# ScalarE of the first mixer product in hand-set order, and the sums of the fourth moving operand in three places

## The chip, the cores and the metric

The kernel runs on one core of one Trainium2 chip. The time is device microseconds (us) of one execution; the figure quoted is the median of several executions. The core has a matrix engine (TensorE, PE in the profile; its weight loads are listed apart as PEld), a vector engine (VectorE, DVE), a scalar engine (ScalarE, ACT), GpSimd (POOL), and DMA queues, of which this kernel mostly uses the one issued from SyncE (SP). Each engine runs its own stream of instructions; where one needs another's result it waits on a semaphore. Matmul results stand in PSUM, which has eight banks of 128 x 512 32-bit numbers. All other tiles stand in SBUF.

## The reference

```python
def _A_ref(x, wqkv, wo):              # linear attention, 32 heads of 32
    q, k, v = ...x @ wqkv...
    phi = lambda t: jnp.where(t > 0, t + 1, jnp.exp(t)) + 1e-6
    pq, pk = phi(q), phi(k)
    kv = jnp.einsum("bhsd,bhse->bhde", pk, v)
    z = jnp.einsum("bhsd->bhd", pk)
    num = jnp.einsum("bhqd,bhde->bhqe", pq, kv)
    den = jnp.einsum("bhqd,bhd->bhq", pq, z)[..., None] + 1e-6
    return (num / den ...) @ wo

def _B_ref(x, w1, b1, w2, b2):        # token-mixing MLP
    h = _layernorm(x, axis=-1)
    u = _gelu(jnp.einsum("bsd,sf->bdf", h, w1) + b1)
    y = jnp.einsum("bdf,fs->bds", u, w2) + b2
    return y.transpose(0, 2, 1)

h = x + _A_ref(_layernorm(x), A_wqkv, A_wo)
out = h + _B_ref(_layernorm(h), B_w1, B_b1, B_w2, B_b2)
```

x is 2048 x 1024 (S x D), w1 is 2048 x 3584 (S x F), w2 is 3584 x 2048, all bf16. The change lies in "mixer 1", the product of w1 with the normalized h and its gelu.

## The kernel before

The program runs attention, then mixer 1, then mixer 2. In the trace mixer 1 lies between about 235 and 400 us. Its moving operand h is kept in SBUF as hE and hO, the even and odd blocks of 128 rows, each 128 x 8 x 1024 in fp16; gelu(u) goes to gE and gO in the same form.

**Seven products in place of eight.** A pair of 128-wide column blocks of w1 is one `Mixer1`. It computes a 2 x 2 block matrix product with seven block products `p1` to `p7` (512 columns each) instead of eight. The stationary sides of products 5, 6, 7 and 3 are sums of blocks of w1, made on VectorE (tiles `sa`, method `asums`); the moving sides 2 to 7 are differences of blocks of hE and hO. The accumulators A, B, C and E are chained: B starts as a copy of A, C as a copy of B, so one engine copies PSUM to PSUM between the products.

**The same once more inside.** Two `Mixer1` form a `Quad`. Products 1, 5, 2 and 3 of the two are again a 2 x 2 block product, and are done by an `Inner` (or `Inner2`, which adds its results to a base already in SBUF): seven products `i1` to `i7`, of four matmuls of 256 columns each. I call the four inners of a quad in1, in5, in2 and in3, in the order in which they run. Their stationary sums are the tiles `is`; their moving sums come from `inner_moving`, where `sums1`, `sums5`, `sums2` and `sums3` each make four 128 x 1024 differences on VectorE, once for the whole of mixer 1: in order, moving sides 7, 5 (in place), 6 and 4. In an inner, PSUM slices a, b, c and e are chained thus: `i1` fills a; ScalarE copies a to b (line 258); `i6` adds to b; ScalarE copies b to c (line 262); `i2` adds to a, which is a result; `i5` fills e; `i7` adds to c, a result; `i3` adds to b, a result; `i4` adds to c once more, a result, after the result of `i7` has been read out of c. Results go through a `sink`: for in1 ScalarE copies to the base t1a and to the PSUM tile B (lines 493 and 494) or VectorE adds and ScalarE copies to B (499); for in5 ScalarE or VectorE writes the shared tile e (502); for in2 and in3 VectorE adds to the base tiles t1a and t (`t3` in the code).

**Interleaving.** `interleave(n, steps, at)` emits an inner n, and between its products it fills in matmuls of 512 columns from a list of steps: the previous quad's product 4 during in1, this quad's products 6 (in5, start of in2) and 7 (rest of in2, in3). A filler that ends a product puts its evacuation (`copy_c`, line 362; gelu, line 419; the VectorE add of e and then gelu) into a list `late`, which is emptied after `i7` and at the end of the inner. Named points in between (`in`, `mid`, `third`, `out`) let the caller emit sums and gelus.

A quad u is one call of `run1`. u runs from 1 to 6; quad 0 is `run_first`, which does its products 1, 2, 7 and 3 whole and only product 5 by an inner. `sums3` is called in u = 1 alone, whole, by `before_third()`, just ahead of in2's interleave and the add into the first base of product 3.

**What sets the order.** Instructions whose call is wrapped by `pin` (`tc.keep_in_program_order`) stay in program order on their engine; for all others a planner chooses the place in their engine's stream. `Held(engine)` wraps an engine so that its calls are pinned while `Held.on` is true. Before the change `dve` and `pe` are such wrappers, and in mixer 1 all matmuls and VectorE instructions are pinned. The ScalarE calls of mixer 1 go to `nc.scalar` and are placed by the planner.

PSUM has four pools of two banks: psw (inner e and c, and A of products 1 and 2), psx (B), psy (C), psz (E, and the inner a and b). w1 comes over the SP queue, one tile of 2 x 1024 KB for each quad, two tiles in flight, and at the end come the first tiles of w2.

Of the kernel before, what the change touches and what calls it, by code (L numbers as in the profile page):

```python
# [10 lines left out]
P = 128  # L11
F32 = mybir.dt.float32
# [10 lines left out]
BANK = 512  # L23
# [7 lines left out]
def kernel(  # L31
# [12 lines left out]
    nc = tc.nc  # L44
# [5 lines left out]
    CW = min(BANK, D)  # L50
# [34 lines left out]
    pin = tc.keep_in_program_order  # L85
# [51 lines left out]
    HW = CW // 2  # L137
# [69 lines left out]
        return {1: b11, 2: b21, 3: b22, 4: t4, 5: b12, 6: t2, 7: t3}, sums  # L207

    class Held:
        on = False  # L210

        def __init__(self, engine, always=False):
            self.engine, self.always = engine, always

        def __getattr__(self, name):
            op = getattr(self.engine, name)
            return (lambda *a, **kw: pin(op(*a, **kw))) if self.always or Held.on else op  # L217

    dve, pe = Held(nc.vector), Held(nc.tensor)
    hv, ht, hs, hd = (Held(e, True) for e in (nc.vector, nc.tensor, nc.scalar, nc.sync))  # L220

    class Inner:
        banks = 4

        def __init__(self, sts, m, mov, tag, sink, sink_sum):
            self.nk, self.mov, self.tag = sts[0].nk // 2, mov, tag
# [23 lines left out]
        def i1(self):  # L250
            ae = psz.tile([P, BANK], F32, tag="z0", bufs=1, name="psI0")
            bc = psz.tile([P, BANK], F32, tag="z1", bufs=1, name="psI1")
            e, c = ae, bc
            if self.banks == 4:
                e, c = (psw.tile([P, BANK], F32, tag="w", name=f"psI{i}") for i in (2, 3))
            self.a, self.e, self.b, self.c = ae[:, 0:HW], e[:, HW:CW], bc[:, 0:HW], c[:, HW:CW]
            self.mm(1, self.a, True)
            nc.scalar.copy(self.b, self.a)  # L258

        def i6(self):  # L260
            self.mm(6, self.b, False)
            nc.scalar.copy(self.c, self.b)

        def i2(self):
            self.mm(2, self.a, False)
# [2 lines left out]
        def i5(self):  # L268
            self.mm(5, self.e, True)
            self.es = cpool.tile([P, HW], F32, tag="es", name="es")  # L270
            nc.scalar.copy(self.es[:], self.e)

        def i7(self):
            self.mm(7, self.c, False)
# [5 lines left out]

        def i4(self):
            self.mm(4, self.c, False)
            self.sink(1, 0, self.c)

    class Inner2(Inner):
        def i5(self):
# [11 lines left out]
    class Product7:  # L298
# [45 lines left out]
        def p1(self):  # L344
            self.begin()
            self.mm(1, self.A, True)
            nc.scalar.copy(self.B[:], self.A[:])

        def shared_tile(self):
            self.e = cpool.tile([P, BANK], F32, tag=f"e{self.p % 2}", name="e1")  # L350
# [1 line left out]
        def p5(self, ks=None):  # L352
            if ks is None or ks[0] == 0:
                self.E = psz.tile([P, BANK], F32, tag=f"z{self.p % 2}", bufs=1, name="psE1")
            self.mm(5, self.E, True, ks)
            if self.whole(ks):
                self.shared_tile()
                nc.scalar.copy(self.e[:], self.E[:])

        def copy_c(self):  # L360
            self.C = psy.tile([P, BANK], F32, tag="y", name="psC1")
            nc.scalar.copy(self.C[:], self.B[:])  # L362

        def p6(self, ks=None, late=None):
            self.mm(6, self.B, False, ks)
# [20 lines left out]
        def p7(self, cut=None):  # L386
            self.mm(7, self.C, False)
            self.parts = [(0, CW, self.C)]
            if cut is not None:
                self.parts = [(0, cut, self.C), (cut, CW, psw.tile([P, BANK], F32, tag="w", name="psC2"))]  # L390
                nc.scalar.copy(self.parts[1][2][:, cut:CW], self.C[:, cut:CW])
            self.evac_shared(1, self.C)

        def p3(self):
# [17 lines left out]
    class Mixer1(Product7):  # L412
# [3 lines left out]

        def evac(self, fh, dh, ps, a=0, b=CW):
            ft = 2 * self.p + fh
            nc.scalar.activation(
                (gE if fh == 0 else gO)[:, self.p, dh * CW + a:dh * CW + b],  # L420
                ps[:, a:b], ACT.Gelu_apprx_tanh, bias=b1_sb[:, ft:ft + 1], scale=1.0,
            )
# [9 lines left out]
        todo = []  # L432
# [49 lines left out]
    class Quad:  # L482
# [7 lines left out]

        def sink1(self, m, h, ps):
            A, B, c = self.sts[m].A, self.sts[m].B, self.cols(h)
            nc.scalar.copy(A[:, c], ps)
            nc.scalar.copy(B[:, c], A[:, c])

        def sum1(self, m, h, ps, es):
            A, B, c = self.sts[m].A, self.sts[m].B, self.cols(h)
            dve.tensor_tensor(A[:, c], ps, es, ALU.add)
            nc.scalar.copy(B[:, c], A[:, c])

        def sink5(self, m, h, ps):
            nc.scalar.copy(self.sts[m].e[:, self.cols(h)], ps)

        def sum5(self, m, h, ps, es):
            dve.tensor_tensor(self.sts[m].e[:, self.cols(h)], ps, es, ALU.add)
# [1 line left out]
        def steps(self, *fs):  # L507
            return [(f, k) for f in fs for k in range(self.sts[0].nk)]

        def interleave(self, n, steps, at={}):  # L510
            t = len(steps)
            cuts = [0, (5 * t + 8) // 16, (9 * t + 8) // 16, (12 * t + 8) // 16, t]

            late = []

            def fill(q):
                for f, part in groupby(steps[cuts[q]:cuts[q + 1]], lambda s: s[0]):
                    f([k for _, k in part], late)

            def flush():  # L520
                while late:
                    late.pop(0)()

            for f in (
                n.i1, "in", 0, n.i6, n.i2, 1, n.i5, n.i7, flush, 2, "mid", n.i3, "third", 3, n.i4, "out", flush,
            ):
                if isinstance(f, int):
                    fill(f)
                else:
                    (at.get(f, nop) if isinstance(f, str) else f)()  # L530

        def asums(self, m):
            if not isinstance(self.sts[0], Mixer1):
# [97 lines left out]
                dve.tensor_tensor(base[:, m, c], ps, base[:, m, c], ALU.add)  # L631
            return sink

        def run1(self, pend, nxt, on_p4, before_third=nop):
            sts = self.sts
            s4, s6, s7 = self.steps(*[st.p4 for st in pend]), self.steps(*[st.p6 for st in sts]), self.steps(*[st.p7_fill for st in sts])
            c6, c7 = 3 * len(s6) // 4, len(s7) // 2

            def starting():
                self.in1.sums(slice(2, 4))  # L640
                self.asums(5)
                self.in5 = Inner(sts, 5, self.mov5, "i5", self.sink5, self.sum5)
                self.in5.sums(slice(0, 2))
                self.asums(6)
                self.t1 = self.base("t1a")
                for s, st in enumerate(sts):
                    st.begin(self.t1[:, s, :])

            self.interleave(self.in1, s4, {"in": starting, "mid": lambda: self.in5.sums(slice(2, 4))})
            self.asums(7)  # L650
            in2 = Inner2(sts, 2, self.mov2, "i1", self.add_to(self.t1), None)
            in2.sums()
            on_p4()
            nxt = nxt()
            for st in sts:
                st.shared_tile()
            self.interleave(self.in5, s6[:c6])
            sts[0].finish()
            self.asums(3)
            self.base3()  # L660
            in3 = Inner2(sts, 3, self.mov3, "i5", self.add_to(self.t3), None)
            in3.sums()
            before_third()
            sts[0].with_shared(sts[0].base3, sts[0].B)
            self.interleave(in2, s6[c6:] + s7[:c7], {
                "third": lambda: sts[0].evac(0, 0, sts[0].A), "out": lambda: sts[1].evac(0, 0, sts[1].A),
            })
            sts[1].with_shared(sts[1].base3, sts[1].B)
            if nxt is not None:
                nxt.begin1()  # L670
            self.interleave(in3, s7[c7:], {
                "third": lambda: sts[0].evac(0, 1, sts[0].base3), "out": lambda: sts[1].evac(0, 1, sts[1].base3),
            })
            return sts, nxt

    def moving(E, O, T2, T3, T4):
# [11 lines left out]
    with ExitStack() as actx:  # L688
# [21 lines left out]
        with ExitStack() as a1:  # L710
# [455 lines left out]
            for q in range(2, NVP):  # L1166
                for R in (KRun, VRun):
                    n = R(q)
                    i = 2 * q + 3 if R is KRun else 2 * q + 4
# [27 lines left out]
            for b in range(NKB):  # L1197
                j0, n = b * KPB, min(KPB, ND - b * KPB)
# [28 lines left out]
        with ExitStack() as a3:  # L1227
# [143 lines left out]
            for n, (u, j) in enumerate(q_units[8:]):  # L1371
# [14 lines left out]
                if n in sums_at:  # L1386
                    cur = next(ahead)
# [44 lines left out]
    psw = ctx.enter_context(tc.tile_pool(name="psw", bufs=NT, space=PSUM, reuse_waits="tile"))  # L1432
# [13 lines left out]
    mov3, sums3 = inner_moving(hO[:, :, CW:D], NSP, inner1, "hi3")  # L1446
    NQ1 = NFP // 2

    def next_load1(u):
        def load():  # L1450
            if u < NQ1:
                load_w1(u, 0)
                load_w1(u, 1)
            else:
                load_w2(0, wpool)
        return load

    def quad1(u):
        return Quad([Mixer1(2 * u), Mixer1(2 * u + 1)], mov1, mov5, mov2, mov3)

    Held.on = True
    sums5()
    cur.mov5 = mov5
    pend, nxt = cur.run_first(quad1(1), sums1, sums2)
    for u in range(1, NQ1):
        cur = nxt
        pend, nxt = cur.run1(pend, lambda: quad1(u + 1) if u + 1 < NQ1 else None, next_load1(u + 1), sums3 if u == 1 else nop)
    Held.on = False
    for st in pend:
        st.p4()  # L1470
    mctx.close()
# [11 lines left out]
    cur = Mixer2(0)  # L1483
# [42 lines left out]
    pend = [cur, Mixer2(1)]  # L1526
    nxt = quad2(1)
# [26 lines left out]
    for u in range(1, NSP // 2):  # L1554
        cur = nxt
        last = 2 * u + 2 == NSP
# [35 lines left out]
```

## Time and profile before

| | us |
|---|---|
| median of 8 runs | 570.06 |
| lowest and highest | 568.27, 570.83 |
| the profiled execution | 570.83 |
| its span, first to last instruction | 569.0 |
| TensorE busy in the span | 560.0 |
| VectorE busy | 431.7 |
| ScalarE busy | 280.9 |

A row of a timeline gives the start of a group of like instructions and its length in us, the engine, the line of the code, the operation, the tile written and those read, the shape, the count, and in brackets how long the engine stood idle before it and what it waited for. Line 217 is the helper that pins, so all pinned matmuls and VectorE instructions have that line and are told apart by their tiles. In in1 to in3 the moving side is hE (in1, in5) or hO (in2, in3), or a sum `hi`; the stationary side is wq (the tile of w1), `sa` or `is`. A matmul's own duration is a latency: of matmuls in a row, those of 512 columns start about 0.217 us apart and those of 256 about 0.109 us apart. The clock of TensorE in a row of a window is 1.00 at full speed.

### The profile page before, as it was taken

The page shows a single profiled execution, that of the slowest core. Times are in us where ns is not written, and L with a number is a line of the kernel's source. Part 1 is how long each engine was busy: PE and PEld are TensorE (multiplying, and loading weights), DVE is VectorE, ACT ScalarE, POOL GpSimd, SP SyncE. Part 2 cuts the span into 40 slices and gives each one's busy share as a digit, 9 for nine tenths or more (in the row PEclk, how much of TensorE's full clock was granted, in tenths as well). Part 3 has the DMA queues.
Part 4 walks back from the last instruction along what each step waited for, and adds up shares of the span by engine and source line. Part 5 has one row for each costly group of instructions (what it writes and reads, how often), then busy time and mean ns, then how long its engine had stood idle before and what let it go on. Part 6 is the DMA issues. An engine that isn't in the chain of part 4 may idle for free.

```text
span 569.0 us, 8564 instructions
## 1 busy us (share of the span) xinstructions
PE 560.0 (98%) x3215; PEld 304.6 (54%) x3215; DVE 431.7 (76%) x822; ACT 280.9 (49%) x597; POOL 1.8 (0%) x8
## 2 busy tenths in 40 slices
PE   8999999999999999999899999999999999999997
PEld 3444444454444444456566666666445655645643
DVE  6898888543785788878889789887989749658725
ACT  4747677757766877635355455464220411311211
POOL 1000000000000000000000000000000000000000
PEclk9999999999999999999899999999999999999999
DMA  9833332125773851104040440413892932912111
GB/s 300 292 75 74 83 85 38 19 66 190 206 217 110 273 181 74 56 0 148 2 149 1 149 127 23 149 55 77 218 245 89 248 90 74 288 47 74 38 47 46
DMA packets 86089, 67.15 MB, mean 118 GB/s; under 512 B 15762, under 2 KB 80032, under 8 KB 86048
## 3 DMA queue, kind: packets, MB, share of 16 engines
q1 hardware_dynamic: 85312, 65.94, 40.3%
q10 hardware_dynamic: 672, 0.66, 0.3%
q8 instruction: 25, 0.41, 0.3%
q14 instruction: 16, 0.13, 0.1%
q0 software_dynamic: 64, 0.01, 0.0%
HBM read 54.54 MB, written 8.91 MB: 112 GB/s over the span
## 4 chain that ended last, share of the span: by engine, by line
PE 87%; DVE 9%; ACT 2%; issue 1%; ACTq 0%; DVEq 0%
PE acc_t L217 18%; PE psI L217 15%; PE psC L217 11%; PE psB L217 10%; PE psA L217 4%; PE psB L854 4%; PE psC L854 4%; PE psA L854 4%; DVE is L217 3%; PE acc_t L778 3%; PE psA L328 2%; PE acc_t L1129 2%; PE psB L328 2%; PE psE L854 2%; DVE sa L217 2%; PE psC L328 2%
## 5 line engine op out<-in xcount | busy, mean ns | idle before, releaser
L217 PEld LDWEIGHTS <-wq 128*128 128x128 bf16 (+1 forms) x629 | 61.1, 98 | 48.3 <-issue 2.7
L217 PEld LDWEIGHTS <-sa 128*128 128x128 f16 x627 | 61.8, 99 | 36.5 <-issue 0.3
L217 PEld LDWEIGHTS <-is 128*128 128x128 f16 x568 | 55.7, 98 | 28.0 <-issue 2.7
L217 PE MATMUL acc_t<-wo_sb,pqT 128*128 128x512 f16 x256 | 55.6, 379 | 0.0
L217 PE MATMUL psC<-gs,wq 128*128 128x512 f16 (+2 forms) x210 | 44.9, 365 | 0.0
L217 PE MATMUL acc_t<-xnT,wq_sb 128*128 128x512 bf16 x192 | 43.4, 379 | 0.0
L217 PEld LDWEIGHTS <-pqT 128*128 128x128 bf16 x256 | 24.9, 98 | 30.5 <-issue 0.6
L179 DVE TENSOR_SCALAR e_sb<-e_sb 128x512 bf16<-128x512 bf16 x64 | 18.6, 290 | 28.7 <-ACT e_sb L175 28.2
L175 ACT ACTIVATE e_sb<-acc_t 128x512 bf16<-128x512 f32 x40 | 23.9, 597 | 24.6 <-PE acc_t L217 12.0
L854 PEld LDWEIGHTS <-xs 128*128 128x128 f16 x208 | 20.0, 98 | 23.3 <-DVE xs L840 1.3
L217 DVE TENSOR_TENSOR ot<-ot,hr 128x512 bf16<-128x512 bf16 (+2 forms) x27 | 11.2, 414 | 28.1 <-ACT ot L469 27.7
L217 PE MATMUL psC<-hT,sa 128*128 128x512 f16 x112 | 31.9, 386 | 0.0
L217 PE MATMUL psI<-hi,is 128*128 128x256 f16 x200 | 30.5, 275 | 0.8 <-ACT psI L258 0.2
L217 PEld LDWEIGHTS <-wq_sb 128*128 128x128 bf16 x192 | 18.5, 98 | 23.0 <-issue 1.3
L258 ACT COPY psI<-psI 128x256 f32<-128x256 f32 x31 | 11.2, 362 | 39.1 <-PE psI L217 38.3
L217 PE MATMUL psB<-hT,sa 128*128 128x512 f16 x112 | 29.7, 379 | 0.0
L217 DVE BATCH_NORM_STATS2 hst<-acc_t 128x6 f32<-128x512 f32 x32 | 21.4, 692 | 9.1 <-ACT h_bf L217 8.9
L854 PE MATMUL psA<-wkv,xnT 128*128 128x512 bf16 x104 | 26.7, 379 | 0.0
L362 ACT COPY psC<-psB 128x512 f32<-128x512 f32 x22 | 12.5, 570 | 25.6 <-PE psB L217 20.9
L854 PEld LDWEIGHTS <-xnT 128*128 128x128 bf16 x156 | 15.3, 98 | 18.5 <-issue 0.2
L217 PE MATMUL psC<-hT,wq 128*128 128x512 f16 x96 | 24.6, 379 | 0.0
L217 ACT CAST h_bf<-acc_t 128x512 bf16<-128x512 f32 x32 | 18.4, 582 | 11.9 <-PE acc_t L217 11.2
(209 smaller groups left out, 1052.7 us busy)
## 6 DMA issues: line engine op xcount, KB each, us to landing
wq<-in_B_w_dram SPq DMA_DIRECT2D x14, 1024.0 KB, 8.0
wq<-in_B_w_dram SPq DMA_DIRECT2D x8, 1792.0 KB, 10.3
xr<-in_A_x_dram SPq DMA_DIRECT2D x16, 256.0 KB, 5.0
rdb<-rd_dram SPq DMA_DIRECT2D x32, 128.0 KB, 3.9
h_dram<-h_bf SPq DMA_DIRECT2D x16, 256.0 KB, 2.0
hr<-h_dram SPq DMA_DIRECT2D x32, 128.0 KB, 2.6
out_dram<-ot SPq DMA_DIRECT2D x31, 128.0 KB, 1.7
x_sb<-in_A_x_dram SPq DMA_DIRECT2D x15, 256.0 KB, 3.0
```

The costliest lines, as they stand in the source:

```text
L175: pin(nc.scalar.activation(e_sb[:], src, ACT.Exp))
L179: pin(nc.vector.tensor_scalar(e_sb[:], e_sb[:], 1.0, PHI_EPS, ALU.min, ALU.add))
L217: return (lambda *a, **kw: pin(op(*a, **kw))) if self.always or Held.on else op
L258: nc.scalar.copy(self.b, self.a)
L328: pe.matmul(ps[:, cols], lhsT=lhs[:, k, :], rhs=mv(k)[:, cols], start=(start and k == 0), stop=(k == self.nk - 1), skip_group_check=True,)
L362: nc.scalar.copy(self.C[:], self.B[:])
L778: mm = nc.tensor.matmul(pp[:, 0:CW], lhsT=xnT[:, kt, i * P:(i + 1) * P], rhs=wkv[:, kt, c * CW:(c + 1) * CW], start=(kt == 0), stop=(kt == ...
L854: pin(nc.tensor.matmul(ps[:], lhsT=lhs[:, k, :], rhs=rhs[:, k, :], start=(start and k == 0), stop=(k == hk2 - 1), skip_group_check=True,))
L1129: nc.tensor.matmul(qp[:, 0:SW], lhsT=wq_sb[:, kt, j * P:(j + 1) * P], rhs=xnT[:, kt, u * SW:(u + 1) * SW], start=(kt == 0), stop=(kt == ND ...
```

## The change

1. **ScalarE in program order.** `Held` takes a key, and a third wrapper `act` pins ScalarE's calls while `Held.scalar` is true, which is so for mixer 1. Every ScalarE copy and gelu of mixer 1 goes through it.
2. **Where evacuations stand in that order.** `late` becomes one list for all quads, so that what is left at the end of an inner can be emitted in the next. `interleave` takes a table `flush`: at which named points (`b` behind i1, `c` behind i6, `7` behind i7, `end`) how many entries are emitted; None is all. in1 empties it at `b` and `7`; in5 at `b`, `7` and `end`; in2 at `7`; in3 one entry at `b` and the rest at `c`. The sink of in1's `i4` and the gelus that stood at `out` of in2 and in3 are put at the head of the list, and are emitted behind the next inner's i1. What is left after the last quad is emitted ahead of its product 4.
3. **The slice c gets its bank at i6** instead of at i1, so that the previous inner's c can still be read behind the next i1. The number of banks is the same.
4. **sums3 in three places** of u = 1: the first two differences ahead of in5, the third between in2 and the add into the second base of product 3, the fourth at `b` of in3.

The core of the diff:

```diff
-            nc.scalar.copy(self.b, self.a)
+            act.copy(self.b, self.a)
         def i6(self):
             self.mm(6, self.b, False)
-            nc.scalar.copy(self.c, self.b)
+            if self.banks == 4:
+                self.c = psw.tile([P, BANK], F32, tag="w", name="psI3")[:, HW:CW]
+            act.copy(self.c, self.b)
...
         def i4(self):
             self.mm(4, self.c, False)
-            self.sink(1, 0, self.c)
+            last = partial(self.sink, 1, 0, self.c)
+            if self.behind is None:
+                last()
+            else:
+                self.behind.insert(0, last)
...
-        def interleave(self, n, steps, at={}):
+        late = []
+        def interleave(self, n, steps, at={}, flush=(("7", None), ("end", None))):
...
+            def point(name):
+                todo = len(self.late) if flush.get(name, 0) is None else flush.get(name, 0)
+                for _ in range(todo):
+                    self.late.pop(0)()
+                at.get(name, nop)()
             for f in (
-                n.i1, "in", 0, n.i6, n.i2, 1, n.i5, n.i7, flush, 2, "mid", n.i3, "third", 3, n.i4, "out", flush,
+                n.i1, "b", 0, n.i6, "c", n.i2, 1, n.i5, n.i7, "7", 2, n.i3, "third", 3, n.i4, "end",
             ):
...
+            self.in1.behind = self.late
+            self.interleave(
+                self.in1, s4, {"b": starting, "7": lambda: self.in5.sums(slice(2, 4))}, (("b", None), ("7", None))
+            )
...
+            if third_sums is not None:
+                third_sums(slice(0, 2))
+            self.interleave(self.in5, s6[:c6], flush=(("b", None), ("7", None), ("end", None)))
...
-            before_third()
             sts[0].with_shared(sts[0].base3, sts[0].B)
-            self.interleave(in2, s6[c6:] + s7[:c7], {
-                "third": lambda: sts[0].evac(0, 0, sts[0].A), "out": lambda: sts[1].evac(0, 0, sts[1].A),
-            })
+            self.interleave(
+                in2, s6[c6:] + s7[:c7], {"third": gelu(0, 0, self.t1), "end": gelu_late(1, 0, self.t1)}, (("7", None),)
+            )
+            if third_sums is not None:
+                third_sums(slice(2, 3))
             sts[1].with_shared(sts[1].base3, sts[1].B)
             if nxt is not None:
                 nxt.begin1()
             self.interleave(in3, s7[c7:], {
-                "third": lambda: sts[0].evac(0, 1, sts[0].base3), "out": lambda: sts[1].evac(0, 1, sts[1].base3),
-            })
+                "b": nop if third_sums is None else lambda: third_sums(slice(3, 4)),
+                "third": gelu(0, 1, self.t3), "end": gelu_late(1, 1, self.t3),
+            }, (("b", 1), ("c", None)))
```

`run_first` is not in the diff: it keeps the default table, and its evacuations are emitted where they stood, but are now pinned.

More of the change, by code (lines that the diff above doesn't have):

```diff
@@ L209, with __init__ @@
     class Held:
-        on = False
-        def __init__(self, engine, always=False):
-            self.engine, self.always = engine, always
+        on = scalar = False
+        def __init__(self, engine, always=False, key="on"):
+            self.engine, self.always, self.key = engine, always, key
         def __getattr__(self, name):
             op = getattr(self.engine, name)
-            return (lambda *a, **kw: pin(op(*a, **kw))) if self.always or Held.on else op
-    dve, pe = Held(nc.vector), Held(nc.tensor)
+            return (lambda *a, **kw: pin(op(*a, **kw))) if self.always or getattr(Held, self.key) else op
+    dve, pe, act = Held(nc.vector), Held(nc.tensor), Held(nc.scalar, key="scalar")
     hv, ht, hs, hd = (Held(e, True) for e in (nc.vector, nc.tensor, nc.scalar, nc.sync))
@@ L223 @@
         banks = 4
+        behind = None
         def __init__(self, sts, m, mov, tag, sink, sink_sum):
@@ L252, in i1 @@
             bc = psz.tile([P, BANK], F32, tag="z1", bufs=1, name="psI1")
[L253 to L256, printed above, removed]
+            e = psw.tile([P, BANK], F32, tag="w", name="psI2") if self.banks == 4 else ae
+            self.a, self.e, self.b, self.c = ae[:, 0:HW], e[:, HW:CW], bc[:, 0:HW], bc[:, HW:CW]
             self.mm(1, self.a, True)
-            nc.scalar.copy(self.b, self.a)
+            act.copy(self.b, self.a)
         def i6(self):
             self.mm(6, self.b, False)
-            nc.scalar.copy(self.c, self.b)
+            if self.banks == 4:
+                self.c = psw.tile([P, BANK], F32, tag="w", name="psI3")[:, HW:CW]
+            act.copy(self.c, self.b)
         def i2(self):
@@ L270, in i5 @@
             self.es = cpool.tile([P, HW], F32, tag="es", name="es")
-            nc.scalar.copy(self.es[:], self.e)
+            act.copy(self.es[:], self.e)
         def i7(self):
@@ L346, in p1 @@
             self.mm(1, self.A, True)
-            nc.scalar.copy(self.B[:], self.A[:])
+            act.copy(self.B[:], self.A[:])
         def shared_tile(self):
@@ L357, in p5 @@
                 self.shared_tile()
-                nc.scalar.copy(self.e[:], self.E[:])
+                act.copy(self.e[:], self.E[:])
         def copy_c(self):
             self.C = psy.tile([P, BANK], F32, tag="y", name="psC1")
-            nc.scalar.copy(self.C[:], self.B[:])
+            act.copy(self.C[:], self.B[:])
         def p6(self, ks=None, late=None):
@@ L390, in p7 @@
                 self.parts = [(0, cut, self.C), (cut, CW, psw.tile([P, BANK], F32, tag="w", name="psC2"))]
-                nc.scalar.copy(self.parts[1][2][:, cut:CW], self.C[:, cut:CW])
+                act.copy(self.parts[1][2][:, cut:CW], self.C[:, cut:CW])
             self.evac_shared(1, self.C)
@@ L418, in evac @@
             ft = 2 * self.p + fh
-            nc.scalar.activation(
+            act.activation(
                 (gE if fh == 0 else gO)[:, self.p, dh * CW + a:dh * CW + b],
@@ L492, in sink1 @@
             A, B, c = self.sts[m].A, self.sts[m].B, self.cols(h)
-            nc.scalar.copy(A[:, c], ps)
-            nc.scalar.copy(B[:, c], A[:, c])
+            act.copy(A[:, c], ps)
+            act.copy(B[:, c], A[:, c])
         def sum1(self, m, h, ps, es):
@@ L498, in sum1 @@
             dve.tensor_tensor(A[:, c], ps, es, ALU.add)
-            nc.scalar.copy(B[:, c], A[:, c])
+            act.copy(B[:, c], A[:, c])
         def sink5(self, m, h, ps):
-            nc.scalar.copy(self.sts[m].e[:, self.cols(h)], ps)
+            act.copy(self.sts[m].e[:, self.cols(h)], ps)
         def sum5(self, m, h, ps, es):
@@ L508, in steps @@
             return [(f, k) for f in fs for k in range(self.sts[0].nk)]
-        def interleave(self, n, steps, at={}):
+        late = []
+        def interleave(self, n, steps, at={}, flush=(("7", None), ("end", None))):
             t = len(steps)
             cuts = [0, (5 * t + 8) // 16, (9 * t + 8) // 16, (12 * t + 8) // 16, t]
-            late = []
+            flush = dict(flush)
             def fill(q):
                 for f, part in groupby(steps[cuts[q]:cuts[q + 1]], lambda s: s[0]):
[L518 to L522, printed above, removed]
+                    f([k for _, k in part], self.late)
+            def point(name):
[3 more added lines that the diff above has]
+                at.get(name, nop)()
             for f in (
-                n.i1, "in", 0, n.i6, n.i2, 1, n.i5, n.i7, flush, 2, "mid", n.i3, "third", 3, n.i4, "out", flush,
+                n.i1, "b", 0, n.i6, "c", n.i2, 1, n.i5, n.i7, "7", 2, n.i3, "third", 3, n.i4, "end",
             ):
@@ L528, in interleave @@
                     fill(f)
+                elif isinstance(f, str):
+                    point(f)
                 else:
-                    (at.get(f, nop) if isinstance(f, str) else f)()
+                    f()
         def asums(self, m):
@@ L632, in add_to, with run1 @@
             return sink
-        def run1(self, pend, nxt, on_p4, before_third=nop):
+        def run1(self, pend, nxt, on_p4, third_sums=None):
             sts = self.sts
@@ L647, in starting, with gelu, gelu_late @@
                     st.begin(self.t1[:, s, :])
-            self.interleave(self.in1, s4, {"in": starting, "mid": lambda: self.in5.sums(slice(2, 4))})
+            def gelu(s, dh, t):
+                return lambda: sts[s].evac(0, dh, t[:, s, :])
+            def gelu_late(*args):
+                return lambda: self.late.insert(0, gelu(*args))
+            self.in1.behind = self.late
+            self.interleave(
+                self.in1, s4, {"b": starting, "7": lambda: self.in5.sums(slice(2, 4))}, (("b", None), ("7", None))
+            )
             self.asums(7)
@@ L656, in run1 @@
                 st.shared_tile()
-            self.interleave(self.in5, s6[:c6])
+            if third_sums is not None:
+                third_sums(slice(0, 2))
+            self.interleave(self.in5, s6[:c6], flush=(("b", None), ("7", None), ("end", None)))
             sts[0].finish()
@@ L1459, in quad1 @@
         return Quad([Mixer1(2 * u), Mixer1(2 * u + 1)], mov1, mov5, mov2, mov3)
-    Held.on = True
+    Held.on = Held.scalar = True
     sums5()
@@ L1466 @@
         cur = nxt
-        pend, nxt = cur.run1(pend, lambda: quad1(u + 1) if u + 1 < NQ1 else None, next_load1(u + 1), sums3 if u == 1 else nop)
-    Held.on = False
+        pend, nxt = cur.run1(pend, lambda: quad1(u + 1) if u + 1 < NQ1 else None, next_load1(u + 1), sums3 if u == 1 else None)
+    while Quad.late:
+        Quad.late.pop(0)()
+    Held.on = Held.scalar = False
     for st in pend:
```

## The prediction

> **What bounds the kernel.** I read the page first: span, busy time, and the row of the clock.
>
> ```profile
> span 569.0 us, 8564 instructions
> PE 560.0 (98%) x3215; PEld 304.6 (54%) x3215; DVE 431.7 (76%) x822; ACT 280.9 (49%) x597; POOL 1.8 (0%) x8
> ...
> PEclk9999999999999999999899999999999999999999
> ```
>
> TensorE sets the time everywhere in mixer 1: ScalarE at half load can only matter where a matmul waits for it. One slice has a lower clock. So the second view is the waits of TensorE alone (us in total, times, longest):
>
> ```profile
> PE psI L217 <- DVE t1a L217: 2.5, 1, 2.5
> PE acc_t L778 <- ACT xnT L1031: 0.9, 2, 0.5
> PE psI L217 <- ACT psI L258: 0.2, 1, 0.2
> ```
>
> Only the first and the third lie in mixer 1. A matmul's listed length is a latency, so short gaps hide in it; the third view is therefore the timeline of TensorE, in which I compare each start with the pitch of 0.217 us (512 columns) and 0.109 us (256 columns). This is u = 1, in2, and then two windows with their clock, the third number from the end:
>
> ```profile
> 272.56 0.81 PE L217 MATMUL psC<-hT,sa 128*128 128x512 f16 x3
> 275.83 0.60 PE L217 MATMUL psI<-hi,wq 128*128 128x256 f16 x4 [2.46 <-DVE t1a L217]
> ```
> ```profile
> 10.80:13.00 2.20, 2.19 (x11) 1.01 (x12) 1.54 (x6) 2.06 (x6) 0.00 (x0) 1.00 1.07 368
> 276.50:279.70 3.20, 3.20 (x15) 1.76 (x13) 2.34 (x5) 2.31 (x5) 0.00 (x0) 0.50 0.00 0
> ```
>
> i4 of in2 starts 2.62 us late, then TensorE runs 3.2 us at clock 0.50. From the psC matmuls at 272.56 to those at 279.89 it takes 7.33 us; the same stretch of u = 2, 299.71 to 302.75, takes 3.04. This one place costs **4.29 us**. The timeline of VectorE shows why:
>
> ```profile
> 270.85 0.69 DVE L217 TENSOR_TENSOR hi<-hO 128x1024 f16<-128x1024 f16 x1
> ...
> 273.02 0.69 DVE L217 TENSOR_TENSOR hi<-hO,hi 128x1024 f16<-128x1024 f16 x1
> 273.63 0.68 DVE L217 TENSOR_TENSOR t<-psB,e 128x512 f32<-128x512 f32 x1
> 274.23 1.87 DVE L217 TENSOR_TENSOR t1a<-psI,t1a 128x256 f32<-128x256 f32 x4
> ```
>
> The four differences of sums3 (0.72, 0.73, 0.72 and 0.61 us to the next start, 2.78 together) stand ahead of in2's adds, and i4 may not write c before i7's add has read it (275.35 to 275.77; i4 starts 0.05 later).
>
> Each later quad is 22.86 us long and has one gap, at i6 of in5. Here u = 3, TensorE and then ScalarE:
>
> ```profile
> 335.39 1.03 PE L217 MATMUL psB<-hT,sa 128*128 128x512 f16 x4
> 336.52 0.60 PE L217 MATMUL psI<-hi,is 128*128 128x256 f16 x4
> ```
> ```profile
> 335.25 0.68 ACT L419 ACTIVATE gO<-psC,b_sb 128x512 f16<-128x512 f32 x1
> 335.84 0.36 ACT L493 COPY t1a<-psI 128x256 f32<-128x256 f32 x1
> 336.09 0.38 ACT L258 COPY psI<-psI 128x256 f32<-128x256 f32 x1
> ...
> 341.07 0.37 ACT L502 COPY e<-psI 128x256 f32<-128x256 f32 x1 [1.17 <-PE psI L217]
> 341.50 0.36 ACT L258 COPY psI<-psI 128x256 f32<-128x256 f32 x1
> 342.42 0.57 ACT L362 COPY psC<-psB 128x512 f32<-128x512 f32 x1 [0.56 <-PE psB L217]
> ```
>
> Four psB matmuls take 0.87 us, so i6 could start at 336.25 and starts at 336.52: **0.27 us**. The copy to b (L258) stood behind a gelu and the sink L493. In u = 1 the same gap is 0.35.
>
> **The change, part by part.**
>
> *sums3, first two differences ahead of in5.* VectorE is idle from 264.18 to 266.32 there (2.14 us, waiting for TensorE); the two take 1.45 and end at 265.6. Nothing waits. Cover gone, each would delay in5's adds one for one. In2's adds now start as in u = 2, where i4 is on time: **-4.29**.
>
> *Third and fourth difference.* Both lie between in2's last add and in3's first. In u = 2 VectorE works through this without idling: add 300.99, e 301.33, t 301.93, two sums, in3's i2 add at 303.32. Two more at 0.61 put it at 304.54. The shift of e's add from first to last of this stretch (it now follows in3's i6) leaves the sum unchanged. Then the i5 add follows after 0.34, i7's after another 0.79 (the distance of these two in in2), 305.67, ending 306.09; i4 of in3 starts 0.05 later, at 306.14 instead of 305.14. The third difference also holds i6 (done 302.02, wanted 301.88: 0.19), inside the same wait. **+1.00**, once. By bounds: 0 if VectorE catches up, 1.00 plus a second spell of half clock, 1.6, if the wait cools the clock.
>
> [...]
>
> *Copy to b first.* With L493, L494 and the gelu behind it, in5's L258 follows the last L499 (done 335.32) and i1 (its last matmul ends 335.56): start 335.6, done 335.96, wanted by 336.20. The gap is gone: 0.35 + 5 x 0.276 = **-1.73**. What was ahead is now behind: L493, L494 and gelu take 0.40 + 0.31 + 0.58 us, and L262 for c ends some 0.25 us later against the matmuls. i7, which waits for it, comes 0.7 us after that. The gelu frees a bank of psC that is written again 5 us later.
>
> *copy_c (L362) of the first half in in5.* It ran when its product ended; it is now emitted at `end`, behind i4's L502 and ahead of in2's L258. On the times above: L502 at 341.07, L362 about 0.28 later (L493 to the next copy took 0.25 to 0.31), L258 0.48 later (the distance from L362 to the next copy at 296.70), done 342.19, i6 at 342.24 instead of 342.17. **+0.07** each, 6 x 0.07 = +0.42 (bounds 0.04 and 0.10 by the pitch). The second half's copy_c goes to `7` of in2, 3 us ahead of its product 7.
>
> *The rest of the order.* The gelus at `third` wait for VectorE now as before; L258 already stands behind them. The gelus and e's add of in3 moved behind i6, and L271 ahead of a gelu, are ScalarE work without a matmul behind it: nothing. Bank c at i6 follows the same turn of two banks: nothing. No DMA moves.
>
> *run_first's end.* This is a loss. The last gelu of quad 0 is emitted ahead of u = 1's i1; the planner had put L258 ahead of it:
>
> ```profile
> 255.15 0.72 ACT L419 ACTIVATE gE<-e,b_sb 128x512 f16<-128x512 f32 x1 [1.26 <-DVE e L217]
> 256.13 0.36 ACT L258 COPY psI<-psI 128x256 f32<-128x256 f32 x1 [0.26 <-PE psI L217]
> 256.48 0.72 ACT L419 ACTIVATE gE<-e,b_sb 128x512 f16<-128x512 f32 x1
> ```
>
> That gelu needs VectorE's add (ends 256.38), so it can't start before 256.48. [...]
>
> **Sum.** -4.29 + 1.00 - 1.73 + 0.42 + 0.50 = **-4.10**. The profiled execution, span 569.0, would have a span of 564.9 and take 570.83 - 4.1 = 566.7. It is the slowest of the eight; from the median, 570.06 - 4.10 = **566.0**.
>
> **Rivals.**
> - *The clock takes part of it back.* in3's wait of 1 us brings a spell of half clock, or the old spell was not in most runs: 1.6 less gain, 567.6. For it: 1 us lies between 0.45 and 2.46. Against: it is nearer to 0.45.
> - *The order does nothing.* L258 stays late because the add into A or the bank of b holds it. Then only the sums and the loss at run_first count: -4.29 + 1.00 + 0.50, 567.3. Against: that add ends at 334.86, 0.7 us before i1 ends.
> - *The wait moves whole.* in3's i4 waits as long and as cold as in2's did, because the two differences also push the adds of i3 and the next quad's sums: no change, 570. Against: 1.22 us added, not 2.78, and two 0.4 us idles behind.
> - *Slower.* Fixed order blocks ScalarE's head in every quad: the gelu at `third` of in2 waits for VectorE's add and holds in3's L258. In u = 2 it starts at 300.50 and frees ScalarE at 301.12; L258 starts 301.43, and i6 has 0.04 to spare, so 0.35 us of VectorE's lag are free, and each further one costs six times. To come out 0.3% slower it must eat 4.1 + 1.7 us, 0.97 a quad, so a lag of 1.3 us: about 572. Against: VectorE idles 1.74 us in in5, which absorbs a lag.
>
> **How the numbers follow.** Forecast 0.60, clock 0.15, order 0.08, wait moves 0.10, slower 0.07. Same means within 0.3%, 1.7 us, about what a measurement of this kernel can tell from no change. The first three are faster: 0.83. The forecast's own range is 565.0 to 567.0, from the bounds of the copies and the spread of the eight. To hold 0.8 it reaches over clock and order, 564.8 to 568.1.
>
> **What would show it.** TensorE's waits: the 2.5 us row on t1a gone, one of some 0.8 us on t before in3's i4 in u = 1, no clock of 0.50 after 240 us. Quads of about 22.65 us. L258 ahead of L493 in in5, and at the end of run_first a gap of 0.5 before psI<-hi,is near 257. I am wrong if VectorE's in2 adds still start late, if in3 shows half clock, or if a quad keeps its 22.86.

## The result, and the profile after

| us | before | changed |
|---|---|---|
| median | 570.06 (32 executions) | 566.27 (11) |
| lowest to highest | 568.27 to 570.89 | 565.97 to 566.79 |
| the profiled execution, its span | 570.83, 569.0 | 566.07, 564.3 |
| first matmul of mixer 1 to first of mixer 2 | 165.41 | 161.37 |

The ratio is 0.9938, with an interval of 0.9927 to 0.9949: 0.6% faster, where -4.10 us, 566.0, was forecast. The last row is the measure I use below, since the time up to mixer 1 differs between executions (235.07 us in the trace before, 234.34 in the one after) though nothing was changed there. That difference arises in the first 7 us, on TensorE: its clock is first recorded at full speed at 6.80 us in the trace before and at 4.13 us in the one after, and two matmuls of 512 columns take 1.03 us ahead of that and 0.61 behind it. First a row of before, then one of after:

```profile
5.16 1.03 PE L98 MATMUL acc_t<-warm 128*128 128x512 bf16 x2
4.74 0.61 PE L98 MATMUL acc_t<-warm 128*128 128x512 bf16 x2
```

Mixer 1 itself became 4.04 us shorter.

The page of the changed kernel:

```profile
span 564.3 us, 8558 instructions
...
PE 557.5 (99%) x3215; PEld 303.5 (54%) x3215; DVE 431.4 (76%) x822; ACT 281.5 (50%) x597; POOL 1.8 (0%) x8
...
PEclk9999999999999999999999999999999999999999
```

The same instructions for VectorE and ScalarE, the same busy time within 0.6 us, and no slice with a lower clock. TensorE's waits, as far as they lie in mixer 1 (in total, times, longest):

```profile
PE psI L217 <- DVE t L217: 0.6, 1, 0.6
PE psI L217 <- ACT psI L217: 0.4, 1, 0.4
```

The 2.5 us on t1a are gone. What came instead are the two waits that the forecast named. In the timeline of TensorE they are the first i6 of u = 1 (five matmuls from 255.20 take 1.08 us, so i6 is 0.51 late) and i4 of u = 1's in3 (0.78 late; the same in3's i6 is 0.20 late, at 274.44), and then the small one at in2's i6, here of u = 2 (0.08 late):

```profile
255.20 1.24 PE L217 MATMUL psC<-hT,wq 128*128 128x512 f16 x5
256.79 0.60 PE L217 MATMUL psI<-hi,is 128*128 128x256 f16 x4 [0.35 <-ACT psI L217]
...
277.28 0.59 PE L217 MATMUL psC<-hT,sa 128*128 128x512 f16 x2
278.49 0.60 PE L217 MATMUL psI<-hi,sa 128*128 128x256 f16 x4 [0.61 <-DVE t L217]
...
291.52 1.03 PE L217 MATMUL psB<-hT,sa 128*128 128x512 f16 x4
292.46 0.60 PE L217 MATMUL psI<-hi,is 128*128 128x256 f16 x4
```

VectorE shows the sums in their three places. In u = 1 the first two stand where it waited for TensorE, the third and fourth between in2's last add and in3's adds:

```profile
263.62 0.68 DVE L217 TENSOR_TENSOR hi<-hO 128x1024 f16<-128x1024 f16 x1
264.34 0.69 DVE L217 TENSOR_TENSOR hO<-hO 128x1024 f16<-128x1024 f16 x1
265.75 0.42 DVE L217 TENSOR_TENSOR e<-psI,es 128x256 f32<-128x256 f32 x1 [0.71 <-PE psI L217]
...
273.70 0.68 DVE L217 TENSOR_TENSOR hi<-hO 128x1024 f16<-128x1024 f16 x1
...
275.69 0.69 DVE L217 TENSOR_TENSOR hi<-hO,hi 128x1024 f16<-128x1024 f16 x1
```

ScalarE: now that its calls are pinned they all have line 217. At the end of `run_first` the copy to b (psI<-psI) follows quad 0's last gelu. In u = 2 it stands ahead of in1's sink in in5, and behind the copy to C in in2:

```profile
255.75 0.72 ACT L217 ACTIVATE gE<-e,b_sb 128x512 f16<-128x512 f32 x1 [0.60 <-DVE e L217]
256.38 0.36 ACT L217 COPY psI<-psI 128x256 f32<-128x256 f32 x1
...
286.07 0.36 ACT L217 COPY psI<-psI 128x256 f32<-128x256 f32 x1 [0.27 <-PE psI L217]
286.34 0.38 ACT L217 COPY t1a<-psI 128x256 f32<-128x256 f32 x1
...
291.28 0.37 ACT L217 COPY e<-psI 128x256 f32<-128x256 f32 x1 [2.02 <-PE psI L217]
291.55 0.59 ACT L217 COPY psC<-psB 128x512 f32<-128x512 f32 x1
292.06 0.35 ACT L217 COPY psI<-psI 128x256 f32<-128x256 f32 x1
```

A quad is now 22.67 us long (278.92 to 301.59, in1 to in1) instead of 22.86.

### The profile page after: what moved, and what is told of

It is laid out like the page before. It is cut to its first block, busy times and chain, and to the rows that moved or that the text cites. A ratio compares the mean times of both kernels' runs of the same rounds, so it can differ in the third digit from the quotient of the medians.

```text
span 564.3 us, 8558 instructions
## 1 busy us (share of the span) xinstructions
PE 557.5 (99%) x3215; PEld 303.5 (54%) x3215; DVE 431.4 (76%) x822; ACT 281.5 (50%) x597; POOL 1.8 (0%) x8
## 4 chain that ended last, share of the span: by engine, by line
PE 94%; DVE 3%; DMA 1%; issue 1%; SPq 1%; ACT 0%; DVEq 0%; ACTq 0%
PE psI L217 19%; PE acc_t L217 18%; PE psC L217 15%; PE psB L217 11%; PE psA L217 4%; PE psB L877 4%; PE psC L877 4%; PE psA L877 4%; PE psB L333 2%; PE acc_t L1152 2%; PE psA L333 2%; PE psE L877 2%; PE psC L333 2%; PE acc_t L801 2%; DMA x_sb<-in_A_x_dram 1%; PE kvps L830 1%
## 5 line engine op out<-in xcount | busy, mean ns | idle before, releaser
L217 ACT COPY psI<-psI 128x256 f32<-128x256 f32 x50 | 17.9, 359 | 11.6 <-PE psI L217 10.5
L176 ACT ACTIVATE r_sb<-acc_t 128x512 bf16<-128x512 f32 x40 | 23.7, 593 | 0.0
```

Source lines behind the costliest of these rows:

```text
L176: pin(nc.scalar.activation(r_sb[:], src, ACT.Relu))
```

## The experiments

No kernel below leaves anything of the computation out. "Stretch" is the last row of the table above, from each run's profile. The kernel before was run beside each set: medians 570.24, 570.52 and 570.54.

### The two halves alone, and two groups of times

`e0_before` is the kernel before, unchanged.

> The kernel before, unchanged, to see the clock of each of its executions. Theory A (the half-clock spell behind the 2.6 us wait comes in some executions only and makes the two groups of times): executions near 568.4 us have a mean clock of 1.000, those near 570.5 us one of 0.997 (3.3 us of 568 at half clock), and no execution lies between with either. Rival B (the two groups come from the start of the kernel or from the memory): the clock is 0.997 in both groups.

`e1_sums_only` is the kernel before with

```diff
+            third_sums(slice(0, 2))
             self.interleave(self.in5, s6[:c6])
...
-            before_third()
...
+            third_sums(slice(2, 3))
             sts[1].with_shared(sts[1].base3, sts[1].B)
...
             self.interleave(in3, s7[c7:], {
+                "in": lambda: third_sums(slice(3, 4)),
```

> The three places of sums3 alone, ScalarE as before. My theory: the wait of 2.6 us and the half clock go, in3 of u = 1 waits 1.0 us in two pieces, and the gaps of 0.27 us at i6 of in5 stay (6), none of 0.5 us at the end of run_first. That is 0.8 us slower than the changed kernel (1.73 - 0.42 - 0.50): 567.1 us, and one group of times only. Rival (the new order of ScalarE does nothing or harm): 565.8 to 566.3.

`e2_order_only` is the changed kernel with

```diff
-            if third_sums is not None:
-                third_sums(slice(0, 2))
             self.interleave(self.in5, s6[:c6], flush=(("b", None), ("7", None), ("end", None)))
...
+            if third_sums is not None:
+                third_sums(slice(0, 4))
             sts[0].with_shared(sts[0].base3, sts[0].B)
```

and without the third and fourth call.

> The new order of ScalarE alone, sums3 whole at its old place. My theory: 3.29 us slower than the changed kernel where the half clock comes, 569.6, and 1.6 less, 568.0, where it doesn't; two groups of times as before, each 0.8 us below the group of the kernel before. The gap at in5's i6 is gone, i6 of in2 has 0.08, the end of run_first 0.51. Rival (the order alone carries the gain): 567 or less.

| | median, us | stretch, us | executions with mean clock 0.997 or less |
|---|---|---|---|
| e0_before | 570.36 | 165.40 | 7 of 12 |
| e1_sums_only | 567.23 | 162.10 | 0 of 6 |
| e2_order_only | 567.86 | 164.59 (with half clock) | 4 of 12 |

The sums alone bring 3.30 us of the stretch, the order alone 0.81, together 4.11 against the 4.04 of both: my 3.29 and 0.81. The rival by which the order carries the gain falls; so does the one by which it does nothing. In e1 the six gaps of 0.28 to 0.35 at in5's i6 are there as before; in3 waits 0.79 at i6 and 0.18 at i4, the same 0.97 in another division, because in that kernel e's add still comes ahead of the third difference. In e2 the wait before in2's i4 is 2.53 us, and in5's i6 is on time.

The two groups of times follow theory A, for the greater part of their distance. In e0 five executions at 568.3 to 568.7 us have clock 1.000 and seven at 570.0 to 570.8 have 0.997. The executions of before beside it split in the same way, apart from two at 569.4 with a clock of 1.000 and one at 573.46 with 0.994. e2 has eight at 567.5 to 568.5 with 0.999 or 1.000 and four at 569.7 to 570.3 with 0.996 or 0.997. Here I had the shares the wrong way round: I gave 569.6 with the half clock as first value, and two thirds were without.

The spell costs 7.33 - 3.04 - 2.62 = 1.67 us, but the groups, about 568.4 and 570.7, lie 2.3 apart. The start of the program, which rival B named, may hold the rest. The four profiled executions with a spell (before, e0, e2, e6) reach mixer 1 at 235.0 to 235.4 us; of the ten without one, seven reach it at 234.3 to 234.6 and three (e4, e7, e11) at 235.0 to 235.6. The mean clock doesn't tell of this, since the clock is listed as 1.00 in the first 6.8 us too. No execution of before without a spell was profiled, so this share is not shown.

### The evacuations ahead of the copy again

`e7_evac_first` is the changed kernel with

```diff
-            self.in1.behind = self.late
             self.interleave(
-                self.in1, s4, {"b": starting, "7": lambda: self.in5.sums(slice(2, 4))}, (("b", None), ("7", None))
+                self.in1, s4, {"b": starting, "7": lambda: self.in5.sums(slice(2, 4))}, (("b", None), ("7", None), ("end", None))
             )
```

> The changed kernel, with one thing turned back: the sink of in1's i4 and what is left of in1's evacuations are emitted at in1's end again, ahead of in5's copy to b, though in fixed order. My theory: L493, L494 and the gelu (0.40 + 0.31 + 0.58 us) stand ahead of the copy, which then starts 1.29 us after the last copy of the sums and comes 0.69 us too late for i6: 6 x 0.69 = +4.1 us, 570.4. Rival (something other than the place in the queue, the bank of b or the add into A, sets that copy): no gap, 566.3.

Measured: 570.78 us, stretch 165.58, so +4.21; the gap at in5's i6 is 0.62 in u = 1 and 0.72 in the five others, 4.22 together. ScalarE in u = 2:

```profile
310.98 0.37 ACT L217 COPY t1a<-psI 128x256 f32<-128x256 f32 x1
311.38 0.38 ACT L217 COPY psB<-t1a 128x256 f32<-128x256 f32 x1
311.69 0.68 ACT L217 ACTIVATE gO<-psC,b_sb 128x512 f16<-128x512 f32 x1
312.27 0.37 ACT L217 COPY psI<-psI 128x256 f32<-128x256 f32 x1
```

It is the place in the queue alone that decides when the copy to b comes: 1.29 us of other work ahead of it, from 310.98 to 312.27, as added up beforehand. It also shows that at this place a fixed order as such gains nothing: in the order in which the kernel before emits these, pinning costs more than the planner's choice did (0.72 against 0.28 us), since the planner had put the copy between the two copies of the sink.

### The three waits that the change left

`e3_all_ahead`: `third_sums(slice(0, 4))` ahead of in5, and none later.

> The changed kernel with all four differences of sums3 ahead of in5. My theory: VectorE waits for TensorE there long enough: the four end about 266.4 on the clock of the changed kernel's trace, in5's add for i7 (now at 265.75) starts 0.65 later and ends 0.1 us before i4 wants it, and the 0.2 us by which it is late further on stays within the room of in2's i4. Both waits of in3 (0.20 and 0.78) go: 0.9 to 1.0 us less, 565.3. Rival (VectorE has no room left ahead of in5): in5's i4 or in2's i4 waits 0.5 to 1 us instead, 565.8 to 566.3.

`e4_copy_c`:

```diff
-            self.interleave(self.in5, s6[:c6], flush=(("b", None), ("7", None), ("end", None)))
+            self.interleave(self.in5, s6[:c6], flush=(("b", None), ("7", None)))
...
-                in2, ... (("7", None),)
+                in2, ... (("b", None), ("7", None))
```

> The changed kernel with the first copy to C emitted behind in2's copy to b instead of at in5's end. My theory: the 0.08 us at in2's i6 goes in each of six quads, 0.48 us less, 565.8. Rival (those 0.08 us are the pipe's own, not the queue's): no difference, 566.3.

`e5_first_gelu`, in `run_first`:

```diff
-            for st in sts:
-                st.p3()
+            sts[0].p3()
+            sts[1].p3_mm()
+            self.late.append(sts[1].p3_evac)
```

> The changed kernel with quad 0's last evacuation put into the list, so that it comes behind the first copy to b of u = 1. My theory: the 0.51 us at the first i6 of u = 1 goes, 565.8. Rival (VectorE's add for that gelu also holds what follows): less than half of it goes, 566.1.

`e6_all_three`: these three together.

> The last three together. If each of the three causes stands by itself: 0.95 + 0.48 + 0.51 = 1.9 us less than the changed kernel, 564.4, and no gap over 0.1 us left in mixer 1. Rival (they share a cause, so that removing one removes part of another): 564.8 or more.

| | median, us | stretch, us | against the changed kernel's stretch |
|---|---|---|---|
| e3_all_ahead | 565.41 | 160.39 | -0.98 |
| e4_copy_c | 578.65 | 172.95 | +11.58 |
| e5_first_gelu | 565.65 | 160.86 | -0.51 |
| e6_all_three | 578.56 | 173.57 (with half clock) | +12.20 |

e3 and e5 give what was expected: both waits of in3 gone without a new one, and the first i6 of u = 1 on time. e4 missed altogether: 0.5 us faster was expected, 12 us slower was measured. Its timelines, of ScalarE and then of VectorE, both in u = 2:

```profile
294.58 0.36 ACT L217 COPY psI<-psI 128x256 f32<-128x256 f32 x1
297.51 0.57 ACT L217 COPY psC<-psB 128x512 f32<-128x512 f32 x1 [2.57 <-DVE t L217]
```
```profile
296.80 0.68 DVE L217 TENSOR_TENSOR t<-psB,e 128x512 f32<-128x512 f32 x1
```

The copy to C reads the PSUM tile B of the first half. So does VectorE's add into the base of product 3, which the program emits between in5 and in2. Moved past that add, the copy waits for its end (297.48; the copy starts at 297.51), although neither writes what the other reads; product 7, filled in behind in2's i2, waits for the copy, 2.01 us in each quad. The trace shows this order of the two readers of B and its price; what enforces it is not shown. I had costed the place by ScalarE's queue alone. e6 holds the same mistake and tells nothing about whether the three causes add up.

`e10_copy_c_third` empties the list in in5 once earlier instead:

```diff
-            self.interleave(self.in5, s6[:c6], flush=(("b", None), ("7", None), ("end", None)))
+            self.interleave(self.in5, s6[:c6], flush=(("b", None), ("7", None), ("third", None), ("end", None)))
```

> The changed kernel with the list also emptied between i3 and i4 of in5, so that the first copy to C stands ahead of i4's copy, and still ahead of VectorE's add of B. My theory of the run that moved it behind in2's copy to b: it lost 2.0 us a quad because the copy was then emitted behind VectorE's add that reads the same B, and had to wait for it; here it isn't, and ScalarE is idle for 2.0 us there. So 0.08 us less in each of six quads, 565.8, and no wait on C. Rival (any other place than in5's end costs): above 566.3.

`e11_all_three_third` is e3, e5 and e10 in one.

> That, together with all four differences ahead of in5 and quad 0's last evacuation behind the first copy to b. If the three causes stand by themselves: 566.27 - 0.48 - 0.86 - 0.62 (the two measured singly) = 564.3, and no gap over 0.1 us left in mixer 1 but perhaps 0.13 at in5's i4 of u = 1. Rival (they share a cause): 564.7 or more.

e10: 565.57 us, stretch 160.90, -0.47; the six gaps of 0.08 are gone and nothing waits for C. That bears out both the 0.08 as the queue's and the explanation of e4, since the copy is again ahead of the add.

e11: 564.83 us, stretch 159.66, -1.71; its ratio to before is 0.9906, interval 0.9893 to 0.9920. It is below both kernels. The three add up to 1.96, so 0.25 is missing. It stands at two new gaps, 0.13 at in5's i4 and 0.14 at in2's i4 of u = 1: with the other waits gone TensorE comes earlier, and the four differences in a row end too late for it by as much. The causes are apart, but the room on VectorE that e3 used was in part made by the other waits. A variant with only three differences ahead was not tried.

### How long a wait TensorE's clock bears

`e8_three_old` and `e9_two_old` are the changed kernel with one difference, or two, ahead of in5, and the rest at the old place ahead of in2's adds.

> The changed kernel with one difference of sums3 ahead of in5 and three at the old place. The wait of in2's i4 in u = 1 is 2.53 us with four there, so about 1.80 with three, and in3 has none. Theory A (the spell of half clock comes with a chance that grows with the wait): 565.4 + 1.8 = 567.2, and 1.6 more in fewer than the four of twelve executions that had it at 2.53. Rival (it comes once the wait passes a length between 1 and 2.5 us): all at 567.2 or a third at 568.8.

> The same with two ahead and two at the old place: a wait of about 1.08 us, 565.4 + 1.1 = 566.5. Both theories of the clock: no spell of half clock, since the 0.98 us of the changed kernel had none in 12 executions. If one shows, the changed kernel was lucky.

Measured: 567.17 and 566.49 us, waits of in2's i4 of 1.80 and 1.08 us. In no execution of either was the clock as low as 0.997.

| wait of TensorE, us | runs | executions with a spell of half clock |
|---|---|---|
| 0.78 to 0.79 | changed kernel, e1, e5, e7, e10 | 0 of 40 |
| 1.08 | e9 | 0 of 6 |
| 1.80 | e8 | 0 of 5 |
| 2.01, six times each | e4 | 0 of 4 |
| 2.32 | e6 | 3 of 5 |
| 2.53 | e2 | 4 of 12 |
| 2.62 | before, all repeats with a listed clock | 44 of 63 |

A spell is read here from a mean clock of 0.997 or less. The wait is the longest single one; the 0.98 us that I took for the changed kernel when I wrote down what e9 should do are its two waits in in3, 0.20 and 0.78, which lie 4 us apart. Both theories had left no spell in e9. For e8 the chance that only grows with the wait and the one with a lower end foretold nearly the same; with e4 added, whose 24 waits of 2.01 us brought none, a lower end between 2.01 and 2.32 us is the better reading, and past it chance.

The traces show where the chance may come in. In all fourteen the clock changes only at whole multiples of 3.413 us after it first reached full speed (79 of them from 6.80 to 276.45 us in the trace before, 78 from 7.20 to 273.44 in e6), and each of the four spells is one such step long. These are the step ahead of the spell before, and the spell. Each row gives the step, its length, TensorE's busy time and matmuls, the clock, and two numbers of the DMA queues:

```profile
273.04:276.45 3.41, 0.95 (x8) 1.00 0.00 0
276.45:279.87 3.42, 3.42 (x15) 0.50 0.01 2
```

Idle time of TensorE below is the step's length less its busy time. It comes out some 0.2 us shorter than the wait counted from starts.

| trace | step begins at, us | TensorE idle in it, us | clock of the next step |
|---|---|---|---|
| before | 273.04 | 2.46 | 0.50 |
| e0 | 272.83 | 2.45 | 0.50 |
| e2 | 273.15 | 2.37 | 0.50 |
| e6 | 270.02 | 2.16 | 0.50 |
| e6 | 321.22, 345.12 | 1.85 each | 1.00 |
| e4 | 270.06, 345.15, 369.04 | 1.85 each | 1.00 |
| e8 | 270.68, 274.09 (one wait over two steps) | 0.98, 0.66 | 1.00 |

So in these traces the clock stayed behind steps with up to 1.85 us of idle time and halved behind those with 2.16 us or more. If it is the idle time within one step that counts, a wait must not only be long enough but also fall into one step: the 2.62 us of the kernel before, cut in half by the end of a step, would leave 1.3 us in each (an estimate), less than what the clock bore. That its executions without a spell are of this kind is not shown, as none was profiled.

## Why the prediction was right

| step | forecast | measured |
|---|---|---|
| sums3 away from in2's adds, with the half clock | -4.29 | both gone from the trace; with in3's wait, -3.30 in e1 |
| in3 of u = 1 waits | +1.00, of it 0.19 at i6 | +0.98: 0.20 at i6, 0.78 at i4 |
| in5's i6 | -1.73 | gaps gone; back in e7 when the queue's order is turned back |
| in2's i6 | +0.42, 0.07 each | 0.08 each; e10 takes 0.47 out |
| end of run_first | +0.50 | +0.51; e5 takes 0.51 out |
| sum | -4.10 | -4.04 in the stretch |

What carried it was counting starts against the pitch of the matmuls instead of reading idle time: of the 6.1 us that mixer 1 lost, 1.7 of them by the half clock, the waits of TensorE listed 2.7. The +0.50 at the end of `run_first` was my estimate for a copy to b that stays behind the gelu emitted ahead of it; no trace of before shows this, as there the copy came first. The changed kernel shows 0.51 in its place: the gelu starts at 255.75, the copy to b 0.63 later, and i6 waits for the copy.

Of the rivals, the one in which the clock takes part back had two halves. The 0.45 us that it is weighed with are TensorE's two waits for xnT in the trace before, 0.45 us ahead of 8.01 and 0.46 ahead of 10.81, behind which the clock stayed at 1.00. In no execution did in3's wait, 0.78 us at the longest, bring half clock, so that half fell. The other, that the old spell was not in most runs, fell too, since it came in 44 of 63; but it did not come in all. The forecast of 566.0 was counted from the median before, and held because most executions behind that median had the spell. Had most been without, near 568.4, the same sum would have given 564.3, 2 us too low; that they were not is luck. Against an execution before without the spell, near 568.4, the change brings 2.1 us and not 3.8; the sum with the 1.6 us of that rival taken off gives 2.5. The 4.04 us of the stretch are no luck: they lie between a trace with the spell and one without, and each term of the sum is found in them.

The one term of mine that was too sure is "the rest of the order: nothing". It was true of the change, but in e4 the place of the copy to C was bound by VectorE's read of the same tile as well as by ScalarE's queue (it started 0.03 us after the add that reads B had ended), and I had looked for the second only.

## What to carry to other kernels

When an engine looks 98% busy, compare its starts with the pitch of the same instructions elsewhere; here that found 6.1 us, half clock included, where the list of waits had 2.7. A queue in program order has to be priced copy by copy (in e7 the copy to b came behind 1.29 us of other work, and i6 was 0.62 to 0.72 us late): what stands ahead of the copy that a matmul waits for, and how much the copy has to spare, and it pays to look also at the edges (first quad, last quad), where the order was written for another case. Sums that are needed once, later, belong where their engine waits, not ahead of adds that free an accumulator.

## What the runs showed of the hardware

TensorE went to half clock for 3.41 us behind a single wait of 2.3 to 2.6 us, in part of the executions (3 of 5 in e6, 4 of 12 in e2, 44 of 63 of the kernel before), and in none behind waits of up to 2.01 us (0 of 4 in e4). In the traces the step of 3.41 us ahead of it held 2.16 us or more of idle time; steps with 1.85 us had no such effect. The four steps that led to a spell were not idle from end to end: TensorE was busy for 0.95 to 1.26 us of each. The spell costs 1.67 us and makes most of the distance between the two groups of times of the kernel before, about 568.4 and 570.7 us.

Two engines that only read one PSUM tile were not free of one another in this program: in e4 the second in program order started 0.03 us after the first had ended, 2.57 us after its own engine was free.
